# GroupNorm on one core: VectorE's loop unrolled over six ring slots, and two programs aligned with `addr_align`

## The chip, the cores and the metric

One core of one Trainium2 chip. The metric is the device time of one execution in microseconds (us). Every kernel is quoted by the median of its runs, with their range. A ratio "after over before" is the mean time of one kernel's fast runs over the mean of the other's fast runs of the same rounds on the same chip, so it is not quite the ratio of the quoted medians; it comes with a 95% interval.

The span of a run is what the profile covers, from the first to the last work on the core.

## The reference

GroupNorm in bf16 over an input of 128 x 1024 x 32 x 16, 32 groups of 32 channels:

```python
xr  = x.reshape(B, G, C // G, H, W)              # B=128, G=32, C=1024, H=32, W=16
mu  = xr.mean(axis=(2, 3, 4), keepdims=True)
var = ((xr - mu) ** 2).mean(axis=(2, 3, 4), keepdims=True)
xn  = (xr - mu) / jnp.sqrt(var + 1e-5)
return xn.reshape(B, C, H, W) * g[None, :, None, None] + b[None, :, None, None]
```

A row of one sample and one group has 32 x 512 = 16384 elements. 128 such rows make a tile of 4 MB, and there are 32 tiles. Every tile is read once and written once.

## The kernel before

Six ring slots of 4 MB hold the tiles. SyncE issues every large load and store into one DMA queue, in runs: some stores in a row, then as many loads in a row. The order is fixed by `RUNS`.

```python
SLOTS = 6
RUNS = (3, 4, 4, 4, 4, 4, 3, 6)
# ... cut ...
        for j in range(1, SLOTS):
            load(j)
        i = 0
        for run in RUNS:
            for n in range(run):
                store(i + n)
            i += run
            for j in range(i + SLOTS - run, min(i + SLOTS, NT)):
                load(j)
```

So the queue carries six loads, then tiles 0 to 2 out (tile 2 in two halves), tiles 6 to 8 in, tiles 3 to 6 out, tiles 9 to 12 in, and so on. A store is issued when VectorE has normalised its tile; a load when the store that last used its slot has landed.

Of a tile, PE sums one half (16 matmuls with an identity matrix), VectorE sums the other half by pairs, ScalarE forms the mean, two passes of squares and the root, and VectorE normalises in place with 32 instructions. ScalarE's program starts with two small loads of 2 KB, the gain and the bias:

```python
    def on_scalar(e):
        e.dma_start(out=gb_b[:, 0:KC], in_=g_v).then_inc(s_gb, 16)
        e.dma_start(out=gb_b[:, KC : 2 * KC], in_=b_v).then_inc(s_gb, 16)
        e.wait_ge(s_ones, 1)
        e.activation(out=warm[:], in_=eps_t[:], func=ACT.Sqrt)
    # ... cut: mean, squares, variance, root of each tile ...
    def on_tensor(e):
        e.wait_ge(s_eye, 2)
        e.wait_ge(s_gb, 32)
        e.matmul(out=gb_p[:], lhsT=rep[:], rhs=gb_b[:], start=True, stop=True).then_inc(s_gbp, 1)
        # ... cut ...
    def on_vector(e):
        # part(i, lo, n): a piece of slot i % SLOTS, at an address computed at run time
        e.wait_ge(s_gbp, 1)
        e.tensor_copy(out=gb[:], in_=gb_p[:])
        pair(0)
        with nc.Fori(0, NT, 1, engines=[e.engine]) as i:
            with e.If(i < NT - 1):
                e.drain()
                pair(i + 1)
            parts = [part(i, k * HW, HW) for k in range(KC)]
            e.keepalive_nop([e.lower_ap(a) for a in parts])
            e.wait_ge(stded, i + 1)
            # ... cut: 1/std, scale, shift, each with its semaphore ...
            for k, a in enumerate(parts):
                ts = e.tensor_scalar(
                    out=a, in0=a, scalar1=scl[:, k : k + 1], scalar2=bia[:, k : k + 1],
                    op0=ALU.mult, op1=ALU.add,
                )
                if (k + 1) % KQ == 0:
                    ts.then_inc(done, 1)
```

Of the kernel before, what the change touches and what calls it, by code (L numbers as in the profile page):

```python
# [8 lines left out]
ALU = mybir.AluOpType  # L9
F32 = mybir.dt.float32  # L10
BF16 = mybir.dt.bfloat16
# [5 lines left out]
SLOTS = 6  # L17
RUNS = (3, 4, 4, 4, 4, 4, 3, 6)
NQ = 4
PS_BUFS = 3  # L20
PE_CHUNKS = 16
MM_FREE = 512


# [33 lines left out]
def kernel(  # L58
# [13 lines left out]
    nc = tc.nc  # L72
# [3 lines left out]
    HW = H * W  # L76
# [3 lines left out]
    NT = B0 // NS  # L80
    KC = C // G
    F = KC * HW
    inv_n = 1.0 / float(F)
    NMM = F // MM_FREE
    ROUNDS = -(-NT // SLOTS)
    REST = NT - (ROUNDS - 1) * SLOTS
    KQ = KC // NQ
    PAIRED = F - PE_CHUNKS * MM_FREE
    ITEM = 2
    assert NT > SLOTS and 0 < REST < SLOTS and sum(RUNS) == NT and RUNS[-1] == SLOTS  # L90
    assert F % MM_FREE == 0 and PAIRED % 2 == 0 and SLOTS % PS_BUFS == 0

# [5 lines left out]
    def sbuf(name, shape, dtype):  # L98
        return nc.alloc_sbuf_tensor(name, shape, dtype)


    ring = sbuf("ring", [P, SLOTS * F], BF16)
    ja = sbuf("ja", [P, F // 2], FP8)
    jm = sbuf("jm", [P, MM_FREE + 1], FP8)
    jp = sbuf("jp", [P, PAIRED // 2], FP8)
# [4 lines left out]
    gb = sbuf("gb", [P, 2 * KC], F32)  # L110
    eps_t = sbuf("eps_t", [P, 1], F32)
    warm = sbuf("warm", [P, 1], F32)
    nm = sbuf("nm", [P, SLOTS], F32)
    sq = sbuf("sq", [P, 2], F32)
    var = sbuf("var", [P, 1], F32)
    std = sbuf("std", [P, SLOTS], F32)
    rstd = sbuf("rstd", [P, 1], F32)
    scl = sbuf("scl", [P, KC], F32)
    bia = sbuf("bia", [P, KC], F32)

    ps = nc.alloc_psum_tensor("ps", [P, PS_BUFS * 2 * MM_FREE], F32)
    gb_p = nc.alloc_psum_tensor("gb_p", [P, 2 * KC], F32)

    def sem(name):
        return nc.alloc_semaphore(name)

    def sems(name):
        return [sem(f"{name}{c}") for c in range(SLOTS)]

    ld, st, summed, meaned = (sems(n) for n in ("ld", "st", "sum", "mean"))  # L130

    half, both, varred = (sems(n) for n in ("half", "both", "var"))
    inverted, scaled, shifted = (sem(n) for n in ("inv", "scl", "bia"))
    first_in, paired, stded, done = (sem(n) for n in ("first", "pair", "std", "done"))
    s_gb, s_ones, s_eye, s_gbp, s_fin = (sem(n) for n in ("gbl", "ones", "eye", "gbp", "fin"))

    def store_parts(i):
# [2 lines left out]
    def slot(i):  # L140
        return ring[:, (i % SLOTS) * F : (i % SLOTS + 1) * F]
# [55 lines left out]
    def in_rounds(e, one):  # L197
        with nc.Fori(0, ROUNDS, 1, engines=[e.engine]) as t:
            for c in range(REST):
                one(c, t)  # L200
            with e.If(t < ROUNDS - 1):
                for c in range(REST, SLOTS):
                    one(c, t)
# [6 lines that stand above are left out]
        e.ldweights(eye[:])  # L210

        def add_up(to, chunk, k):
            return e.add_instruction(  # L213
                mybir.InstMatmult(
                    name=nc.get_next_instruction_name(),
                    engine=e.engine,
                    start_tensor_calc=(k == 0),
                    stop_tensor_calc=(k == PE_CHUNKS - 1),
                    ins=[e.lower_ap(chunk), e.lower_ap(eye[:])],
                    outs=[e.lower_ap(to)],  # L220
                    tile_size=(P, P),
                    tile_position=(0, 0),
                    ldweights=False,
                )
            )

        def one(c, t):
            for k in range(PE_CHUNKS):
                if k == 0:
                    e.wait_ge(ld[c], (t + 1) * 16)  # L230
                elif k == PE_CHUNKS - 2:

                    e.wait_ge(meaned[(c - 2) % SLOTS], t + 1)
                elif k == PE_CHUNKS - 1:
                    e.wait_ge(paired, t * SLOTS + (c + 1))
                mm = add_up(sums(c), slot(c)[:, k * MM_FREE : (k + 1) * MM_FREE], k)
                if k == 0:
                    mm.then_inc(first_in, 1)
            mm.then_inc(summed[c], 1)

        in_rounds(e, one)

    def on_scalar(e):
        e.dma_start(out=gb_b[:, 0:KC], in_=g_v).then_inc(s_gb, 16)
        e.dma_start(out=gb_b[:, KC : 2 * KC], in_=b_v).then_inc(s_gb, 16)
        e.wait_ge(s_ones, 1)
        e.activation(out=warm[:], in_=eps_t[:], func=ACT.Sqrt)  # L247

        def one(c, t):
            e.wait_ge(summed[c], t + 1)  # L250
            e.activation(  # L251
                out=jm[:], in_=sums_and_pairs(c), func=ACT.Identity, scale=-inv_n,
                accum_out=nm[:, c : c + 1], saturate=False,
            ).then_inc(meaned[c], 1)
            for h, (ready, at) in enumerate(
                ((meaned[c], t + (2 if c >= SLOTS - 2 else 1)), (half[c], t + 1))
            ):
                e.wait_ge(ready, at)
                e.activation(  # L259
                    out=ja[:],  # L260
                    in_=slot(c)[:, h * (F // 2) : (h + 1) * (F // 2)],
                    func=ACT.Square,
                    bias=nm[:, c : c + 1],
                    scale=1.0,
                    accum_out=sq[:, h : h + 1],
                    saturate=False,
                ).then_inc((half, both)[h][c], 1)
            e.wait_ge(both[c], t + 1)
            e.activation(  # L269
                out=var[:], in_=sq[:, 0:1], func=ACT.Identity, bias=eps_t[:], scale=inv_n  # L270
            ).then_inc(varred[c], 1)
            e.wait_ge(varred[c], t + 1)
            e.activation(  # L273
                out=std[:, c : c + 1], in_=sq[:, 1:2], func=ACT.Sqrt, bias=var[:], scale=inv_n
            ).then_inc(stded, 1)

        in_rounds(e, one)

    def on_vector(e):
        bytes_of_ring = ring[:].bitcast(mybir.dt.uint8)  # L280

        def part(i, lo, n):
            at = (i % SLOTS) * (F * ITEM) + lo * ITEM
            return bytes_of_ring[:, bass.ds(at, n * ITEM)].bitcast(BF16)

        def pair(i):
            lo, n = PE_CHUNKS * MM_FREE, PAIRED // 2
            e.wait_ge(first_in, i + 1)
            e.scalar_tensor_tensor(  # L289
                out=jp[:],  # L290
                in0=part(i, lo, n),
                scalar=1.0,
                in1=part(i, lo + n, n),
                op0=ALU.mult,
                op1=ALU.add,
                accum_out=ps[:, bass.ds((i % PS_BUFS) * (2 * MM_FREE) + MM_FREE, 1)],
                saturate=False,
            ).then_inc(paired, 1)

        e.wait_ge(s_gbp, 1)  # L300
        e.tensor_copy(out=gb[:], in_=gb_p[:])  # L301
        pair(0)
        with nc.Fori(0, NT, 1, engines=[e.engine]) as i:
            with e.If(i < NT - 1):
                e.drain()  # L305
                pair(i + 1)
            parts = [part(i, k * HW, HW) for k in range(KC)]
            e.keepalive_nop([e.lower_ap(a) for a in parts])  # L308
            e.wait_ge(stded, i + 1)
            e.reciprocal(out=rstd[:], in_=std[:, bass.ds(i % SLOTS, 1)]).then_inc(inverted, 1)  # L310
            e.wait_ge(inverted, i + 1)
            e.tensor_scalar(  # L312
                out=scl[:], in0=gb[:, 0:KC], scalar1=rstd[:], scalar2=None, op0=ALU.mult
            ).then_inc(scaled, 1)
            e.wait_ge(scaled, i + 1)
            e.scalar_tensor_tensor(  # L316
                out=bia[:], in0=scl[:], scalar=nm[:, bass.ds(i % SLOTS, 1)],
                in1=gb[:, KC : 2 * KC], op0=ALU.mult, op1=ALU.add,
            ).then_inc(shifted, 1)
            e.wait_ge(shifted, i + 1)  # L320
            for k, a in enumerate(parts):
                ts = e.tensor_scalar(  # L322
                    out=a, in0=a, scalar1=scl[:, k : k + 1], scalar2=bia[:, k : k + 1],
                    op0=ALU.mult, op1=ALU.add,
                )
                if (k + 1) % KQ == 0:
                    ts.then_inc(done, 1)

    with entry_block(tc) as entry:
        first_load(nc.sync)  # L330
# [3 lines left out]
        at = next(k for k, i in enumerate(rest) if is_drain(i) and i.engine == load_0.engine)  # L334
# [36 lines left out]
```

## Time and profile before

| | before |
|---|---|
| device time, first three runs | 630.39 us (630.19 to 630.68) |
| profiled span | 629.1 us |
| DMA share of the main queue | 99.3% |
| first tile store issued | 45.9 us |

The prediction below shows the lines from which the DMA bound is read (columns of a timeline: start and duration in us, engine, line, instruction; of the waits: who waits for whom, then total us, count, longest; of windows: window and length, busy us and count of PE, its weight loads, VectorE, ScalarE, GpSimd, then granted clock, DMA share, GB/s).

```profile
0.80 0.40 ACTq L244 DMA_DIRECT2D gb_b<-in_g_dram  x1
1.23 0.50 ACTq L245 DMA_DIRECT2D gb_b<-in_b_dram  x1
```

```profile
144.37 0.33 SPq L164 DMA_DIRECT2D out_dram<-ring  x1
144.74 14.54 SPq L158 DMA_DIRECT2D ring<-in_x_dram  x4
```

### The profile page before, as it was taken

Reading aid. Unit: us, or ns where it says so; the run is one execution under the profiler, and the core shown is the slowest. Engines: PE = TensorE matmul, PEld = TensorE weight load, DVE = VectorE, ACT = ScalarE, POOL = GpSimd, SP = SyncE. Lnnn points to the kernel's source line nnn. Section 1 sums busy time; section 2 is a strip of 40 time slices with the busy share of each in tenths; the row PEclk is TensorE's granted clock in tenths of the full one; section 3 lists DMA queues with packets and bytes.
Section 4 is the critical chain, followed back from the end, with each engine's and each line's share of the span. In section 5 each row is a group of like instructions: output and inputs, shape, how many; then the busy total and the mean of one; then the engine's idle time right before and its main releaser. Section 6 shows DMA issues by size and latency. Waiting matters only on the chain.

```text
span 629.1 us, 2702 instructions
## 1 busy us (share of the span) xinstructions
PE 187.5 (30%) x508; PEld 0.2 (0%) x2; DVE 497.2 (79%) x1185; ACT 504.0 (80%) x258; POOL 1.0 (0%) x8
## 2 busy tenths in 40 slices
PE   2533333430243303433024330343303333063000
PEld 0000000000000000000000000000000000000000
DVE  1479999999499982999829998299983999899962
ACT  0899999999589992999929999299991999979940
POOL 0000000000000000000000000000000000000000
PEclk9867766665577755777557775577755866577555
DMA  9999999999999999999999999999999999999996
GB/s 400 433 433 400 433 433 433 433 433 433 431 433 433 433 433 433 433 425 433 433 433 433 433 431 433 433 433 433 433 433 433 433 431 431 433 427 433 433 419 270
DMA packets 9888, 268.44 MB, mean 427 GB/s; under 512 B 1184, under 2 KB 1184, under 8 KB 1184
## 3 DMA queue, kind: packets, MB, share of 16 engines
q1 hardware_dynamic: 9792, 268.44, 99.3%
q10 hardware_dynamic: 96, 0.00, 0.0%
HBM read 134.22 MB, written 134.22 MB: 427 GB/s over the span
## 4 chain that ended last, share of the span: by engine, by line
ACT 32%; DVE 25%; DMA 24%; issue 9%; PE 4%; DVEq 3%; SPq 0%; ACTq 0%
ACT ja L259 30%; DVE ring L322 23%; DMA ring<-in_x_dram 22%; PE ps L213 4%; DMA gb_b<-in_b_dram 2%; ACT jm L251 1%; DVEq L305 1%; DVEq L308 1%; DVE jp L289 1%; ACT var L269 1%; ACT std L273 1%; DVE bia L316 1%; DVE scl L312 1%; DVEq L289 0%; DVE rstd L310 0%
## 5 line engine op out<-in xcount | busy, mean ns | idle before, releaser
L259 ACT ACTIVATE ja<-ring,nm 128x8192 fp8e5<-128x8192 bf16 x64 | 455.8, 7122 | 2.1
L322 DVE TENSOR_SCALAR ring<-ring,scl,bia x1024 | 333.7, 409 | 1.2
L213 PE MATMUL ps<-ring,eye 128*128 128x512 bf16 x507 | 187.3, 543 | 389.3 <-DVE jp L289 235.1
L289 DVE SCALAR_TENSOR_TENSOR jp<-ring 128x4096 fp8e5 (+1 forms) x32 | 141.6, 4425 | 80.9 <-PE ps L213 68.9
L251 ACT ACTIVATE jm<-ps 128x513 fp8e5<-128x513 f32 x32 | 19.2, 601 | 95.3 <-PE ps L213 95.3
L310 DVE RECIPROCAL rstd<-std 128x1 f32 x32 | 5.7, 177 | 19.3 <-ACT std L273 19.2
L259 ACT ACTIVATION_READ_ACCUMULATOR ja<-ring,nm 128x1 f32 x64 | 11.9, 186 | 0.0
L316 DVE SCALAR_TENSOR_TENSOR bia<-scl,nm,gb 128x32 f32<-128x32 f32 x32 | 8.0, 251 | 4.2
L301 DVE COPY gb<-gb_p 128x64 f32<-128x64 f32 x1 | 0.2, 225 | 12.8 <-PE gb_p L208 12.8
L273 ACT ACTIVATE std<-sq,var 128x1 f32<-128x1 f32 x32 | 9.4, 294 | 1.0
L269 ACT ACTIVATE var<-sq,eps_t 128x1 f32<-128x1 f32 x32 | 9.4, 295 | 1.0
L312 DVE TENSOR_SCALAR scl<-gb,rstd 128x32 f32<-128x32 f32 x32 | 7.7, 242 | 1.1
L251 ACT ACTIVATION_READ_ACCUMULATOR jm<-ps 128x1 f32 x32 | 6.2, 194 | 0.0
L289 DVE DVE_READ_ACCUMULATOR jp<-ring (+1 forms) x32 | 4.5, 142 | 0.0
L208 PE MATMUL gb_p<-gb_b,rep 32*128 32x64 bf16 x1 | 0.2, 208 | 12.5 <-DMA gb_b<-in_b_dram 12.5
L247 ACT ACT_TABLE_LOAD x1 | 1.3, 1283 | 1.8 <-PEq L355 1.8
L190 POOL TENSOR_SCALAR_AFFINE_SELECT rep<-ones_b 32x128 bf16<-32x128 bf16 x1 | 0.3, 303 | 0.0
L186 POOL TENSOR_SCALAR_AFFINE_SELECT eye<-ones_b 128x128 bf16<-128x128 bf16 x1 | 0.3, 293 | 0.4 <-issue 0.4
L247 ACT ACTIVATE warm<-eps_t 128x1 f32<-128x1 f32 x1 | 0.2, 203 | 0.0
L180 POOL MEMSET ones_b<- 128x128 bf16 x1 | 0.2, 204 | 0.3 <-POOLq L355 0.3
L210 PEld LDWEIGHTS <-eye 128*128 128x128 bf16 x1 | 0.1, 105 | 0.1
L208 PEld LDWEIGHTS gb_p<-gb_b,rep 32*128 32x128 bf16 x1 | 0.1, 100 | 12.5 <-issue 12.5
(5 smaller groups left out, 0.5 us busy)
## 6 DMA issues: line engine op xcount, KB each, us to landing
ring<-in_x_dram SPq DMA_DIRECT2D x32, 4096.0 KB, 36.8
out_dram<-ring SPq DMA_DIRECT2D x30, 4096.0 KB, 26.9
out_dram<-ring SPq DMA_DIRECT2D x2, 2048.0 KB, 12.5
out_dram<-ring SPq DMA_DIRECT2D x4, 1024.0 KB, 9.2
gb_b<-in_g_dram ACTq DMA_DIRECT2D x1, 2.0 KB, 7.8
gb_b<-in_b_dram ACTq DMA_DIRECT2D x1, 2.0 KB, 11.1
```

The lines of the kernel that those rows point to most:

```text
L213: return e.add_instruction(mybir.InstMatmult(name=nc.get_next_instruction_name(), engine=e.engine, start_tensor_calc=(k == 0), stop_tensor ...
L251: e.activation(out=jm[:], in_=sums_and_pairs(c), func=ACT.Identity, scale=-inv_n, accum_out=nm[:, c : c + 1], saturate=False,).then_inc(me ...
L259: e.activation(out=ja[:], in_=slot(c)[:, h * (F // 2) : (h + 1) * (F // 2)], func=ACT.Square, bias=nm[:, c : c + 1], scale=1.0, accum_out= ...
L269: e.activation(out=var[:], in_=sq[:, 0:1], func=ACT.Identity, bias=eps_t[:], scale=inv_n).then_inc(varred[c], 1)
L273: e.activation(out=std[:, c : c + 1], in_=sq[:, 1:2], func=ACT.Sqrt, bias=var[:], scale=inv_n).then_inc(stded, 1)
L289: e.scalar_tensor_tensor(out=jp[:], in0=part(i, lo, n), scalar=1.0, in1=part(i, lo + n, n), op0=ALU.mult, op1=ALU.add, accum_out=ps[:, bas ...
L305: e.drain()
L308: e.keepalive_nop([e.lower_ap(a) for a in parts])
L310: e.reciprocal(out=rstd[:], in_=std[:, bass.ds(i % SLOTS, 1)]).then_inc(inverted, 1)
L312: e.tensor_scalar(out=scl[:], in0=gb[:, 0:KC], scalar1=rstd[:], scalar2=None, op0=ALU.mult).then_inc(scaled, 1)
L316: e.scalar_tensor_tensor(out=bia[:], in0=scl[:], scalar=nm[:, bass.ds(i % SLOTS, 1)], in1=gb[:, KC : 2 * KC], op0=ALU.mult, op1=ALU.add,). ...
L322: ts = e.tensor_scalar(out=a, in0=a, scalar1=scl[:, k : k + 1], scalar2=bia[:, k : k + 1], op0=ALU.mult, op1=ALU.add,)
```

## The change

The intent is to take the loop turn, the run-time addresses and the drain off VectorE: the loop body handles the six slots with addresses fixed at build time, so it grows from 54 to 224 instructions (my count of the built program). The loop is aligned with `addr_align(FETCH)`, where `FETCH` is 128, and the code that runs once is put behind it and entered first. ScalarE's 49 instructions are aligned in the same way. That this alignment suits the fetching of instructions was my assumption; what the trace of before shows of fetches is nine packets of 8192 bytes, all outside the span. The counter semaphores become one per slot (54 semaphores become 78), and the pair sum waits for the load itself instead of PE's first matmul.

```diff
+FETCH = 128
-    inverted, scaled, shifted = (sem(n) for n in ("inv", "scl", "bia"))
-    first_in, paired, stded, done = (sem(n) for n in ("first", "pair", "std", "done"))
+    half, both, varred, inverted, scaled, shifted = (
+        sems(n) for n in ("half", "both", "var", "inv", "scl", "bia")
+    )
+    done = sem("done")
 ... cut: paired and stded become one per slot, PE's increment of first_in goes ...
     def on_scalar(e):
+        e.addr_align(FETCH, max_nops=0)
         e.dma_start(out=gb_b[:, 0:KC], in_=g_v).then_inc(s_gb, 16)
         e.dma_start(out=gb_b[:, KC : 2 * KC], in_=b_v).then_inc(s_gb, 16)
 ... cut ...
     def on_vector(e):
+        e.addr_align(FETCH, max_nops=0)
+        ahead = nc.cur_bb
+        nc.br("vector_fetch", engines=[e.engine])
+        nc.switch_bb("vector_start", parent=ahead)
+        def pair(c, turn):
+            e.wait_ge(ld[c], turn * 16)
 ... cut: the same pair sum, with static addresses ...
-        with nc.Fori(0, NT, 1, engines=[e.engine]) as i:
-            with e.If(i < NT - 1):
-                e.drain()
-                pair(i + 1)
-            parts = [part(i, k * HW, HW) for k in range(KC)]
-            e.keepalive_nop([e.lower_ap(a) for a in parts])
+        def one(c, t):
+            then = (c + 1) % SLOTS, t + (1 + (c + 1) // SLOTS)
+            if c == REST - 1:
+                with e.If(t < ROUNDS - 1):
+                    pair(*then)
+            else:
+                pair(*then)
 ... cut: 1/std, scale, shift, 32 normalising instructions on slot(c) ...
+        e.wait_ge(paired[0], 1)
+        in_rounds(e, one)
+        nc.br("vector_end", engines=[e.engine])
+        with nc.body("vector_fetch", parent=ahead, valid_engines=[e.engine]):
+            e.wait_ge(s_gbp, 1)
+            e.tensor_copy(out=gb[:], in_=gb_p[:])
+            pair(0, 1)
+            nc.br("vector_start", engines=[e.engine])
+        nc.switch_bb("vector_end")
```

## The prediction

What no trace of this case showed is cut from the text below and from two expectations (e8, e10), and each cut is marked. Among it is what the first rival was said to cost (a number of fetches in each round, and a time with them). The sum itself is 630.4 - 0 (VectorE) + 0 to 0.3 us (fetches), taken as 630.2 us. Of the fetch term, the 8 KiB and the 0.31 us are read from before's trace (packets of 8192 bytes, the undisturbed ones 307 to 324 ns); their number, one or two, was my estimate and does not follow from a trace.

> **What bounds the kernel now.** I read the page first: engine shares, then the slices, then the DMA queue. No compute engine is near full, but the DMA queue is.
>
> ```profile
> PE 187.5 (30%) x508; PEld 0.2 (0%) x2; DVE 497.2 (79%) x1185; ACT 504.0 (80%) x258; POOL 1.0 (0%) x8
> ...
> DMA  9999999999999999999999999999999999999996
> GB/s 400 433 433 400 433 433 433 433 433 433 431 433 433 433 433 433 433 425 433 433 433 433 433 431 433 433 433 433 433 433 433 433 431 431 433 427 433 433 419 270
> ...
> q1 hardware_dynamic: 9792, 268.44, 99.3%
> ```
>
> The reader is to see a flat 433 GB/s from the first slice to the one before the last. One tile is 4.194 MB in and 4.194 MB out, so at 433 GB/s a tile costs 8.389/433 = 19.37 us of DMA, and 32 tiles cost 619.9 us of the 629.1 us span. Only 9.2 us are left that any change of instructions could touch without moving fewer bytes.
>
> Next I read the waits, of the DMA queue's own engine and of all engines, because the chain of waits is mostly ACT (32%) and DVE (25%) and would mislead here: it follows what released each store, not whether the queue was ever empty.
>
> ```profile
> SPq L164 <- DVE ring L322: 472.9, 31, 42.4
> SPq L158 <- DMA out_dram<-ring: 112.0, 15, 9.6
> SPq L177 <- DMA out_dram<-ring: 11.1, 1, 11.1
> ...
> DVE jp L289 <- PE ps L213: 68.9, 8, 13.5
> DVE rstd L310 <- ACT std L273: 19.2, 16, 6.9
> ...
> DVE jp L289 <- issue: 12.0, 24, 0.5
> ```
>
> SyncE waits 472.9 us for VectorE before it issues stores. That looks like a VectorE bound, but in the table of DMA issues a 4 MB store lands 26.9 us (median) after its issue while it takes 9.7 us to move: about 17 us of earlier transfers stand ahead of it. A store issued some microseconds sooner only waits longer in the queue.
>
> Last, the timeline of VectorE and the end of the run in windows (columns: window and length, then busy us and count of each engine, granted clock, DMA share, GB/s).
>
> ```profile
> 555.29 0.20 DVE L310 RECIPROCAL rstd<-std 128x1 f32 x1
> ...
> 556.19 10.43 DVE L322 TENSOR_SCALAR ring<-ring,scl,bia  x32
> 567.12 4.43 DVE L289 SCALAR_TENSOR_TENSOR jp<-ring 128x4096 fp8e5 x1 [0.50 <-issue]
> ```
>
> ```profile
> 616.00:618.00 2.00, 0.00 (x0) 0.00 (x0) 0.64 (x2) 0.00 (x0) 0.00 (x0) 0.50 0.98 414
> ...
> 622.00:623.00 1.00, 0.00 (x0) 0.00 (x0) 0.00 (x0) 0.00 (x0) 0.00 (x0) 0.50 0.91 385
> 623.00:624.00 1.00, 0.00 (x0) 0.00 (x0) 0.00 (x0) 0.00 (x0) 0.00 (x0) 0.50 0.22 90
> ...
> 626.00:627.00 1.00, 0.00 (x0) 0.00 (x0) 0.00 (x0) 0.00 (x0) 0.00 (x0) 0.50 0.06 25
> 627.00:628.00 1.00, 0.00 (x0) 0.00 (x0) 0.00 (x0) 0.00 (x0) 0.00 (x0) 0.50 0.04 16
> ```
>
> The VectorE lines show a tile's cycle: from one pair-sum start at 550.94 to the next at 567.12 it is 16.18 us, 3.2 us less than the DMA needs. The window lines show two things. VectorE is done at 616.65, yet the DMA stays full for another 6 us: the last stores wait for the queue, not for VectorE. And from 624 us the share is 0.12, then 0.06, which is one engine of sixteen. So the span ends with one slow DMA engine that works alone from about 625 to 628.
>
> From the 16 semaphore increments of each transfer in the trace I followed that engine's distance behind the median of the sixteen: 0.37 us at 129 us, 1.39 at 245, 2.6 at 333, 3.7 at 478, 4.63 at the last store. It grows by about 0.1 us with every store, and by nothing with a load (1.39, 1.39, 1.40 over three loads from 245 to 265 us), apart from one jump of 0.7 us near 273.
>
> [...]the median increment of the last store is at 623.46 us and the last at 628.09.
>
> [...]The trace agrees with fetching by DMA[...]: its DMA records hold nine 8192-byte packets of the instruction kind[...], six before the first instruction, three after the last, and none in the 629 us between. Undisturbed ones took 307 to 324 ns. So the kernel before fetches nothing while it runs.
>
> [...]The trace has 0.50 us of issue time at the loop's turn, for a drain, two branches and register work together.
>
> **The change part by part.**
> Removed: per tile on VectorE, the drain, the loop turn, the dynamic addresses and the keepalive. The row of issue waits has 12.0 us in 24 turns, 0.5 us each; I expect 0.1 to 0.2 left, so 0.3 to 0.4 us of 32 tiles, 10 to 13 us of VectorE time in all. It takes the cycle from 16.2 to about 15.8 us. All of it lies beside a 19.37 us DMA tile: on the path, 0.
>
> Not changed: the 32 normalising instructions of a tile (10.43 us, 326 ns apart), the pair sum (4.43 us) and the three small ones. If static addresses also made issue faster, the 326 ns could shrink; no row of before tells, and it would be hidden too.
>
> Moved: the pair sum waits for the load itself and not for PE's first matmul. PE spent 235.1 us waiting for that sum, so PE and ACT may run some tenths of a microsecond earlier. Hidden, as ACT's cycle is about 16 us (2 squares of 7.25 us, 0.8 for the mean, 0.6 for the rest).
>
> Added: program. The loop grows from 54 instructions to 224 on VectorE (my count of the built program). [...]ScalarE's 49 instructions are only shifted. At the least one or two more 8 KiB fetches on some DMA engine, 0.31 us each; the start of VectorE's real work is at 12.75 us, so a fetch in the first microseconds is hidden.
>
> Sum: 630.4 - 0 (VectorE) + 0 to 0.3 (fetches, if they meet the slow engine). I take 630.2: the median, with a tenth or two off for a little less disturbance where loads turn to stores.
>
> **The rivals.**
> First, the loop is fetched anew in every round. [...]Against: the stall has 3.2 us per tile and a queue of 17 us to hide in, and an engine that is not the slow one stands more than 4 us ahead of it (two stand about 3). So 0 to 1 us[...].
>
> Second, the slow engine is slow because of something that the change removes, so that the tail of 4.6 us shrinks: 626 to 628. For it: the tail is the largest thing in the 9.2 us. Against: its delay comes in steps of 0.1 us with stores only, not in steps of 0.31 us once a round, and no fetch is recorded in the run.[...]
>
> Third, VectorE is on the path at the end: the last tile's work (605.35 to 616.65) delays the last store. Then 0.3 us could be gained, and a fetch stall would cost in full. Against: the queue is full to 622 us, so more than 4 us are spare.
>
> Fourth, the bubbles at load-to-store turns (the slice at 47 to 63 us with 400 GB/s lost about 1 us) change, since stores are issued at other moments: 1 us either way.
>
> **Range and chances.** The three times of before span 0.5 us. The bubbles give about 1 us either way, the second rival stretches downwards, the first a little upwards: 628.2 to 631.8. For 2% (12.6 us) down, more than the whole 9.2 us beside the transfers would have to go, which can't be; for 2% up, VectorE would have to fall behind the DMA by over 3 us in most tiles. Chances: 0.01 faster, 0.975 within 2%, 0.015 slower.
>
> **What would show it.** VectorE's issue wait before the pair sum falls from 12.0 us to under 5; its busy time stays near 497. The slices stay at 433 GB/s and the store's time to landing stays near 27 us or grows. The shares after 623 us keep their 0.06: if they are gone, my second rival is right. If instruction packets of 8192 bytes appear inside the run, the first rival's mechanism exists, and the slow engine's distance tells whether it counts. I'd be wrong altogether if slices in the middle fell under 420, which would mean that VectorE's stalls had emptied the queue.

## More of the kernel before

Where an experiment gives one span, it is that of its profiled run.

I number the large transfers from 0: loads 0 to 5, stores 6 to 9, loads 10 to 12, stores 13 to 16, loads 17 to 20. Transfer 16 is the store of tile 6.

```profile
PE gb_p L208 <- DMA gb_b<-in_b_dram: 12.5, 1, 12.5
```

ScalarE issues the two small loads in half a microsecond each, and the second lands late enough that PE starts only at 12.5 us. With it the work on the tiles begins.

```profile
117.00:119.00 2.00, 2.00 (x7) 0.00 (x0) 1.96 (x7) 1.90 (x3) 0.00 (x0) 0.50 0.84 360
...
148.00:150.00 2.00, 0.59 (x1) 0.00 (x0) 1.83 (x5) 1.01 (x4) 0.00 (x0) 0.50 1.07 459
...
158.00:160.00 2.00, 0.00 (x0) 0.00 (x0) 2.00 (x7) 2.00 (x1) 0.00 (x0) 0.50 0.87 377
...
197.00:199.00 2.00, 0.00 (x0) 0.00 (x0) 2.00 (x8) 1.97 (x3) 0.00 (x0) 1.00 0.91 393
```

In the timeline of SyncE's sequencer, the first line is the store of tile 6 alone, the second the four loads behind it. The store is issued by 144.70 us (144.37 + 0.33). By the semaphore increments in the trace, the store ahead of it lands at 148.56 us (median of its sixteen increments). So transfer 16 stands in the queue only 3.86 us before the queue would have nothing left. I call this distance the margin of a store. Of the stores before those of the last six tiles it is the smallest. The last store of each later run of four has 5.0 to 7.5 us, and the second half of tile 2 (transfer 9) has 6.73. Windows of 2 us swing by a packet or two, since the tool books a packet's bytes at its start; the four windows, at the store of tile 6 and at the turns from loads to stores before and after it, show a queue that does not stop.

```profile
144.84 4.42 DVE L289 SCALAR_TENSOR_TENSOR jp<-ring 128x4096 fp8e5 x1 [0.50 <-issue]
169.64 4.42 DVE L289 SCALAR_TENSOR_TENSOR jp<-ring 128x4096 fp8e5 x1 [9.13 <-PE ps L213]
```

The pair sums from 46 to 145 us wait only for issue: seven tiles in a row (2 to 8) are bound by compute, and what is late at their start is late at their end. The one at 169.64 us waits 9.13 us, for PE's first matmul on a tile whose load has just landed. From there on the queue sets VectorE's clock, and a late start is forgotten.

## The result, and the profile after

| | before | after |
|---|---|---|
| device time, six runs each, same chip | 630.29 us (630.10 to 630.72) | 631.73 us (631.09 to 632.80) |
| ratio after over before | | 1.0025 [1.0012, 1.0038] |
| time outside the span, mean | 1.52, 1.58 and 1.60 us (nine runs on each of three later chips) | 1.90 us (six runs) |

The changed kernel is 0.25% slower: within 2%, but clearly apart, and above what I had allowed. The means of the runs are 631.93 and 630.36 us (the latter from the before runs of the same chip), 1.57 us apart. About 0.3 to 0.4 of it lies outside the span, which leaves about 1.2 us in the span. The profiled run of after was its slowest (632.80 us, span 630.9; the other five spans are 629.2 to 630.8), and the profiled span of before is 629.1, so what is read from these two traces, 1.8 us in the span, is larger than what a typical run lost.

The page of after, in the lines that answer to those of before (the rows with a q are a queue and its kind: packets, MB, share of the 16 engines' time):

```profile
PE 183.8 (29%) x508; PEld 0.2 (0%) x2; DVE 495.7 (79%) x1185; ACT 503.2 (80%) x258; POOL 1.0 (0%) x8
...
GB/s 397 432 432 403 432 426 432 422 434 432 407 432 428 432 432 432 432 432 432 432 432 432 432 432 430 432 432 430 434 432 436 432 428 432 432 436 432 436 423 279
...
q1 hardware_dynamic: 9792, 268.44, 99.3%
...
q14 instruction: 3, 0.02, 0.0%
```

The queue is as full as before, with slices of 426, 422, 407 and 428 where before had 431 to 433. Each slice is 15.8 us long, so these lie at about 79 to 95, 110 to 126, 158 to 174 and 189 to 205 us. A new row counts three instruction packets inside the span; before had none.

VectorE did gain what the change is for. The timeline of one tile's cycle, and the waits of SyncE, follow:

```profile
516.30 4.45 DVE L294 SCALAR_TENSOR_TENSOR jp<-ring 128x4096 fp8e5<-128x4096 bf16 x1
...
521.72 10.43 DVE L327 TENSOR_SCALAR ring<-ring,scl,bia 128x512 bf16<-128x512 bf16 x32
532.03 4.45 DVE L294 SCALAR_TENSOR_TENSOR jp<-ring 128x4096 fp8e5<-128x4096 bf16 x1
```

```profile
SPq L170 <- DVE ring L327: 472.5, 31, 48.0
SPq L164 <- DMA out_dram<-ring: 113.1, 14, 9.4
```

From pair sum to pair sum it is 15.73 us instead of 16.18, and the issue wait of 12.0 us before the pair sum has no row any more. Yet SyncE's waits for VectorE are the same to half a microsecond in total (472.5 for 472.9), and its longest wait, the one for the first store (the last number of the line), grew from 42.4 to 48.0 us. That points to the start of the run:

```profile
1.24 6.12 ACTq L249 DMA_DIRECT2D gb_b<-in_g_dram  x1
7.38 0.44 ACTq L250 DMA_DIRECT2D gb_b<-in_b_dram  x1
```

```profile
PE gb_p L214 <- DMA gb_b<-in_b_dram: 17.5, 1, 17.5
```

The issue of the first small load takes 6.12 us instead of 0.40. The second goes out at 7.38 us instead of 1.23, its data land about 5 us later, PE starts at 17.5 us instead of 12.5, and the first tile store is issued at 51.5 us instead of 45.9. Inside the 6.12 us lie two of the three instruction packets (at 5.29 and 5.62 us; 309 ns each; 8192 bytes). They went to the DMA while the first tile loads were under way: six had been issued by 3.17 us, and the first of them landed at 12.13 us (median of its sixteen increments). One of the two belongs to VectorE's alignment, as e1 and e2 below tell (packets at 5.68 and 11.40 us without ScalarE's alignment, a single one at 5.41 with it alone).

What a late start does to a queue that is "full" is seen at the store of tile 6 (the columns are those of before):

```profile
147.62 0.33 SPq L170 DMA_DIRECT2D out_dram<-ring  x1
147.99 14.49 SPq L164 DMA_DIRECT2D ring<-in_x_dram  x4
```

```profile
117.00:119.00 2.00, 0.00 (x0) 0.00 (x0) 2.00 (x1) 2.00 (x1) 0.00 (x0) 0.50 0.95 262
...
148.00:150.00 2.00, 0.00 (x0) 0.00 (x0) 2.00 (x1) 2.00 (x1) 0.00 (x0) 0.50 0.80 344
...
158.00:160.00 2.00, 0.00 (x0) 0.00 (x0) 2.00 (x8) 2.00 (x1) 0.00 (x0) 0.50 0.69 295
...
197.00:199.00 2.00, 1.19 (x5) 0.00 (x0) 2.00 (x7) 2.00 (x1) 0.00 (x0) 0.90 0.53 229
```

The store is issued 3.25 us later than in before. Of the 5.6 us that the first store was late, the shorter cycle has made good 2.3 by then. The margin of tile 6's store is 1.52 us instead of 3.86; that of transfer 9 is 1.72 us instead of 6.73. And the window at 117 us moved 262 GB/s for 360 in before, those at 158 and 197 us 295 and 229 for 377 and 393.

The margin of tile 6 is 1.52 us, that of transfer 9 is 1.72. The landings tell what this costs. I took the median of the sixteen increments of every large transfer from the two traces:

| transfer | what | lands, before, us | after minus before, us |
|---|---|---|---|
| 11 | load of tile 7 | 109.82 | -0.04 |
| 12 | load of tile 8 | 119.54 | +0.81 |
| 15 | store of tile 5 | 148.56 | +0.91 |
| 16 | store of tile 6 | 158.62 | +1.16 |
| 17 | load of tile 9 | 167.91 | +1.27 |
| 19 | load of tile 11 | 187.33 | +1.27 |
| 20 | load of tile 12 | 197.03 | +1.94 |
| 28 | load of tile 16 | 274.69 | +1.87 |
| 36 | load of tile 20 | 352.26 | +1.80 |
| last | last store | 623.46 | +1.87 |

The loss comes in three pieces: 0.85 us between transfers 11 and 12, where loads give way to stores; 0.36 us from transfer 15 to 17, at tile 6's store; 0.67 us between 19 and 20, the next turn from loads to stores. At the first and the last of these the trace shows 32 KiB packets of up to 2.8 and 3.0 us where one takes 1.21 otherwise; the packets of before take no more than 1.41 us at those turns. By the packets no DMA engine of after stands idle around these places: summed over the sixteen engines, there is no gap from 76 to 122 us or from 140 to 204 us. So the queue of after never ran dry; what it lost, it lost in packets that took longer.

So all that after lost at the median engine it lost before 200 us, and it stayed lost. The distance of the slowest engine behind the median at the last store is 4.83 us, for 4.63 in before. The tail is as long, but not of one engine alone:

```profile
625.00:626.00 1.00, 0.00 (x0) 0.00 (x0) 0.00 (x0) 0.00 (x0) 0.00 (x0) 0.50 0.19 82
...
628.00:629.00 1.00, 0.00 (x0) 0.00 (x0) 0.00 (x0) 0.00 (x0) 0.00 (x0) 0.50 0.12 49
```

Shares of 0.19 and 0.12 are three engines and two, where before had one at 0.06. At the store of tile 29 the three slowest stand 4.91, 4.09 and 3.06 us behind the median, for 4.54, 1.71 and 1.31 in before.

### The profile page after: what moved, and what is told of

The parts are those of the page before. It is cut to its first block, busy times and chain, and to the rows that moved or that the text cites. A ratio compares the mean times of both kernels' runs of the same rounds, so it can differ in the third digit from the quotient of the medians.

```text
span 630.9 us, 2170 instructions
## 1 busy us (share of the span) xinstructions
PE 183.8 (29%) x508; PEld 0.2 (0%) x2; DVE 495.7 (79%) x1185; ACT 503.2 (80%) x258; POOL 1.0 (0%) x8
## 3 DMA queue, kind: packets, MB, share of 16 engines
q1 hardware_dynamic: 9792, 268.44, 99.3%
## 4 chain that ended last, share of the span: by engine, by line
ACT 35%; DMA 34%; DVE 20%; PE 6%; issue 1%; ACTq 1%; SPq 0%; DVEq 0%
ACT ja L264 32%; DMA ring<-in_x_dram 22%; DVE ring L327 16%; DMA out_dram<-ring 11%; PE ps L219 6%; DVE jp L294 3%; DMA gb_b<-in_b_dram 2%; ACT jm L256 1%; ACTq L249 1%; ACT var L274 1%; ACT std L278 1%; DVE bia L320 0%; DVE scl L316 0%; DVE rstd L314 0%; SPq L170 0%
## 5 line engine op out<-in xcount | busy, mean ns | idle before, releaser
L327 DVE TENSOR_SCALAR ring<-ring,scl,bia 128x512 bf16<-128x512 bf16 x1024 | 333.7, 420 | 1.2
L219 PE MATMUL ps<-ring,eye 128*128 128x512 bf16 x507 | 183.6, 535 | 388.4 <-DVE jp L294 227.7
L294 DVE SCALAR_TENSOR_TENSOR jp<-ring 128x4096 fp8e5<-128x4096 bf16 x32 | 142.1, 4440 | 64.5 <-DMA ring<-in_x_dram 64.5
L314 DVE RECIPROCAL rstd<-std 128x1 f32<-128x1 f32 x32 | 5.5, 170 | 35.4 <-ACT std L278 34.3
L339 DVE COPY gb<-gb_p 128x64 f32<-128x64 f32 x1 | 0.2, 225 | 17.7 <-PE gb_p L214 17.7
L214 PE MATMUL gb_p<-gb_b,rep 32*128 32x64 bf16 x1 | 0.2, 207 | 17.5 <-DMA gb_b<-in_b_dram 17.5
L294 DVE DVE_READ_ACCUMULATOR jp<-ring 128x1 f32 x32 | 5.2, 162 | 0.0
L214 PEld LDWEIGHTS gb_p<-gb_b,rep 32*128 32x128 bf16 x1 | 0.1, 100 | 17.5 <-issue 17.5
```

The lines of the kernel that those rows point to most:

```text
L219: return e.add_instruction(mybir.InstMatmult(name=nc.get_next_instruction_name(), engine=e.engine, start_tensor_calc=(k == 0), stop_tensor ...
L294: e.scalar_tensor_tensor(out=jp[:], in0=slot(c)[:, first : first + w], scalar=1.0, in1=slot(c)[:, first + w : first + 2 * w], op0=ALU.mult ...
L314: e.reciprocal(out=rstd[:], in_=std[:, c : c + 1]).then_inc(inverted[c], 1)
L327: ts = e.tensor_scalar(out=a, in0=a, scalar1=scl[:, k : k + 1], scalar2=bia[:, k : k + 1], op0=ALU.mult, op1=ALU.add,)
```

## The experiments

The theory after reading the two traces: **the late start.** ScalarE's alignment makes it jump to instructions that, I supposed, are not yet loaded; the fetch of them, I supposed further, waits among the load packets (e4 below corrects this); the small loads go out 6 us late; all compute is 5 us late; the margins of the early stores are used up, and the queue loses time there and at the turns that follow. The rivals: **the fetches**, which cost the DMA engine that serves them, through VectorE's alignment as much as ScalarE's; and **the static loop**, which by itself issues stores at less favourable moments. In the expectations these stand under their own names: theory F is the alignment's fetch at ScalarE's start, with a late-start branch and an engine branch; rival S is the static loop; theory M says that late work uses up the margin of a store; rival T that a late start costs by itself at the turns. (They speak of a stall of the second small load; the traces show it in the issue of the first.)

Kernel before was run with each group on the same chip: 630.55 us (nine runs) with e1 to e4, 630.66 with e5 to e8, 630.49 with e9 to e11. All kernels gave correct results.

### e1: the change without ScalarE's alignment

```diff
     def on_scalar(e):
-        e.addr_align(FETCH, max_nops=0)
         e.dma_start(out=gb_b[:, 0:KC], in_=g_v).then_inc(s_gb, 16)
```

> The changed kernel without ScalarE's alignment; VectorE's static loop and its alignment stay. Theory F (the fetch at ScalarE's start: it stalls the second gain/bias load for 6 us and two 8 KiB instruction packets set DMA engines back): no 6 us issue on ScalarE, at most one instruction packet inside the span, the early distance of the slowest DMA engine back to about 0.3 us from 1.5, time 630.1 to 630.6. Rival S (the static VectorE loop itself, or its own fetches, cost the time): 631.3 to 632, as the changed kernel. Part of both: the time outside the span stays 0.3 us above before, if it comes from the added semaphores.

Measured: 631.28 us (630.93 to 631.49), ratio 1.0009 [0.9995, 1.0023], span 629.5. That lies above theory F's 630.6 and just under rival S's 631.3. The two issues are back at 0.40 and 0.53 us, PE starts at 14.2 us, and the margin of tile 6 is 3.70 us. The median landing of the last store is 0.40 us earlier than in before, so the loss in the queue is gone. But the time is 0.7 us above before's median, because the slowest engine ends 5.67 us behind the median, a microsecond more than in before. It is 2.04 us behind already early in the run (0.3 was expected), after the two remaining instruction packets (5.68 and 11.40 us; one at most was expected). An engine that far behind would also explain why PE does not start at 12.5 us: the last completion of the two small loads comes at 13.59 us, the one before it at 12.14, for 11.97 and 11.89 in before. So the late start explains the queue's loss; this kernel keeps something else, at its end, and its interval does not tell that from nothing.

### e2: before, with ScalarE's alignment alone

```diff
     def on_scalar(e):
+        e.addr_align(128, max_nops=0)
         e.dma_start(out=gb_b[:, 0:KC], in_=g_v).then_inc(s_gb, 16)
```

> The kernel before with ScalarE's alignment added, nothing else. Theory F: the 6 us stall at the second gain/bias load appears, one or two instruction packets in the first 12 us, time 631.0 to 632. Rival S: the stall may appear, but the time stays at 630.1 to 630.7.

Measured: 632.64 us (631.69 to 633.07), ratio 1.0029 [1.0015, 1.0042], span 631.2. One line, which changes no arithmetic and no order, costs 2.1 us, a little more than the 632 expected at most. The issue in the timeline, and the window at tile 6's store:

```profile
1.23 5.72 ACTq L245 DMA_DIRECT2D gb_b<-in_g_dram  x1
```

```profile
148.00:150.00 2.00, 0.00 (x0) 0.00 (x0) 1.50 (x5) 2.00 (x1) 0.00 (x0) 0.60 0.00 0
```

The stall is there with a single instruction packet (at 5.41 us); PE starts at 16.7 us. With the old loop the margin is -0.40 us: the store comes after the previous one has landed, and no packet starts in these 2 us. The median landing of the last store is 3.52 us later than in before, the slowest engine 3.25 us behind it. The loss therefore doesn't need the static loop, which if anything softens it (1.4 us in after).

### e3: before, with the second small load late and no fetch

```diff
         e.dma_start(out=gb_b[:, 0:KC], in_=g_v).then_inc(s_gb, 16)
+        e.wait_ge(s_gb, 16)
         e.dma_start(out=gb_b[:, KC : 2 * KC], in_=b_v).then_inc(s_gb, 16)
```

> The kernel before, in which ScalarE waits for its first small load to land before it issues the second: the first tile's work starts at about 17.5 us and not 12.7, as in the changed kernel, but nothing is fetched. If the late start is what costs (theory F, late-start branch): 631 to 632, with bubbles where loads turn to stores. If the fetch packets' delay of single DMA engines is what costs (theory F, engine branch): 630.1 to 630.7 and no early distance of 1.5 us.

Measured: 631.89 us (631.25 to 632.39), ratio 1.0017 [1.0003, 1.0031], span 630.7. PE starts at 16.3 us. The margin of tile 6 is -0.43 us and the queue runs dry without a single fetch (by the packets, the engines stand idle for 1.3 us on average):

```profile
148.00:150.00 2.00, 0.00 (x0) 0.00 (x0) 1.50 (x3) 2.00 (x1) 0.00 (x0) 0.50 0.62 262
...
158.00:160.00 2.00, 0.00 (x0) 0.00 (x0) 2.00 (x8) 2.00 (x1) 0.00 (x0) 0.50 0.46 180
```

The landings shift by +1.54 us at transfer 16, +1.99 at 17 and +2.96 at 20, and stay at +2.92 to the end. So being late is enough. Two further things are seen. The loss has another part at the next turn from loads to stores, near 196 us, 0.95 us by the excess of its packets, although the margins there are back above 20 us. And not all of it reaches the end: the slowest engine is only 3.39 us behind at the last store, 1.24 less than in before, so a dry queue also lets the slow engine catch up.

### e4: the change, with ScalarE's alignment behind the two small loads

```diff
     def on_scalar(e):
-        e.addr_align(FETCH, max_nops=0)
         e.dma_start(out=gb_b[:, 0:KC], in_=g_v).then_inc(s_gb, 16)
         e.dma_start(out=gb_b[:, KC : 2 * KC], in_=b_v).then_inc(s_gb, 16)
+        e.addr_align(FETCH, max_nops=0)
         e.wait_ge(s_ones, 1)
```

> The changed kernel with ScalarE's two small loads issued ahead of the alignment: the fetch stays, but the first tile no longer starts late (12.7 us). Late-start branch: back to 630.1 to 630.7. Engine branch: stays at 631.2 to 632, with the early distance of 1.5 us. Rival S: stays as well, even without that distance.

Measured: 630.68 us (630.43 to 631.22), ratio 1.0004 [0.9990, 1.0017], span 628.5: level with before.

```profile
0.80 0.40 ACTq L248 DMA_DIRECT2D gb_b<-in_g_dram  x1
```

```profile
q14 instruction: 3, 0.02, 0.0%
```

```profile
158.00:160.00 2.00, 0.00 (x0) 0.00 (x0) 1.13 (x4) 2.00 (x1) 0.00 (x0) 0.50 0.95 410
```

It makes the same number of fetches, at nearly the same moments (5.64, 5.81 and 11.36 us), and even keeps a slow engine 1.97 us behind early in the run. Only the small loads no longer stand behind the alignment: PE starts at 14.2 us (not at the expected 12.7, as in e1), and the margins of transfers 9 and 16 are 6.09 and 4.90 us. After is 1.44 us above its own before, this kernel 0.13 us above its own, so 1.3 of the 1.44 us come from the order of three lines (the interval of e4 is 0.8 us to each side). This is the clearest of the runs: it keeps the fetches and the static loop, and takes away most of the late start. It also corrects the theory in one place. After the alignment's branch, which the trace has at 1.76 us, ScalarE goes on at once:

```profile
2.20 1.28 ACT L252 ACT_TABLE_LOAD   x1 [2.20 <-issue]
```

That is 0.44 us after the branch and 3.4 us before the first instruction packet, so ScalarE did not stand waiting for the instructions to which it jumped. In e2 too the branch (0.79 us) is followed after 0.44 us by the issue of the small load; it is this issue that then takes 5.72 us.

### e5: the late start of e3, with the run of stores shortened

If the loss is the fourth store of the second run, an order that asks for three stores there should not lose it.

```diff
-RUNS = (3, 4, 4, 4, 4, 4, 3, 6)
+RUNS = (3, 3, 4, 4, 4, 4, 4, 6)
 ... and the wait of e3 ...
```

> The kernel with the late second load (which cost 1.3 us) with one more change: the second run of stores has three instead of four, so that the store of tile 6 no longer has to be issued before 149 us with an almost empty queue. Theory M (late work eats the queue's margin at that store, 3.9 us in the kernel before, none with the late start): the queue does not run dry near 149 to 160 us, slices there back at 433 GB/s, time 630.2 to 631.0. Rival T (a late start costs by itself, through the load-to-store turns near 117 and 197 us): time stays at 631.3 to 632.4.

Measured: 630.67 us (630.33 to 631.26), ratio 1.0001 [0.9987, 1.0014], span 629.3. The start is as late as in e3, and the loss is gone: at transfer 62 the landing is 0.05 us earlier than in before, where e3 is 2.91 us later. The new order changes the end as well (the queue empties among the last stores, and the engines end within 0.47 us of each other), so the last 10 us are not comparable, but in this kernel, whose margin at transfer 9 was still 3.00 us, the loss before 200 us is a matter of that one store. This rests on the landings: the intervals of e3's and e5's ratios overlap.

### e6: before, later still

```diff
         e.dma_start(out=gb_b[:, 0:KC], in_=g_v).then_inc(s_gb, 16)
+        e.wait_ge(ld[0], 16)
         e.dma_start(out=gb_b[:, KC : 2 * KC], in_=b_v).then_inc(s_gb, 16)
```

> Dose: the kernel before with the second small load held until the whole first tile has landed (12.2 us), so the first tile's work starts at about 20 us, 7 to 8 us late instead of 5. Theory M: each further microsecond beyond the margin costs one: the store of tile 6 is issued 2 to 3 us later than with the first dose, time 634 to 636. Rival T: the loss does not grow with the dose, 631.5 to 632.7.

Measured: 636.71 us (636.52 to 637.17, four fast runs), ratio 1.0098 [1.0082, 1.0113]; more than I expected, because I had counted on tile 6's store. The window shows a queue that is dry already at the halves of tile 2:

```profile
80.00:82.00 2.00, 0.57 (x3) 0.00 (x0) 2.00 (x7) 2.00 (x1) 0.00 (x0) 1.00 0.00 0
```

The margins of transfers 7 to 9 are 0.58, -0.90 and 0.68 us, and the landings shift by +2.25 us at transfer 8, +3.36 at 10, +5.74 at 16 and +7.03 at 20, then no more. Beyond the first margin, being late costs on more than one turn.

### e7: the change, with the run of stores shortened

```diff
-RUNS = (3, 4, 4, 4, 4, 4, 3, 6)
+RUNS = (3, 3, 4, 4, 4, 4, 4, 6)
```

> The changed kernel with the second run of stores cut to three as well. Theory M: the 0.4 us at 150 to 170 us are gone, time 630.6 to 631.3 with about 0.3 us of it outside the span. Rival T: 631.5 to 632.5, bubbles near 117 and 197 us remain.

Measured: 631.58 us (630.54 to 632.94), ratio 1.0011 [0.9997, 1.0024]. Inconclusive: by its time it falls to rival T (631.5 to 632.5), by its interval it may be level with before. The loss between 149 and 170 us is nearly gone and so is the one near 197, but the one near 117 us stays (1.0 us, after a margin of 1.51 us at transfer 9), and the slowest engine is 5.9 us behind at the store of tile 29. The runs spread over 2.4 us.

### e8: the static loop alone, with neither alignment

```diff
     def on_scalar(e):
-        e.addr_align(FETCH, max_nops=0)
 ...
     def on_vector(e):
-        e.addr_align(FETCH, max_nops=0)
-        ahead = nc.cur_bb
-        nc.br("vector_fetch", engines=[e.engine])
-        nc.switch_bb("vector_start", parent=ahead)
 ...
+        e.wait_ge(s_gbp, 1)
+        e.tensor_copy(out=gb[:], in_=gb_p[:])
+        pair(0, 1)
         e.wait_ge(paired[0], 1)
         in_rounds(e, one)
-        nc.br("vector_end", engines=[e.engine])
-        with nc.body("vector_fetch", parent=ahead, valid_engines=[e.engine]):
 ... the four lines of the entry block, now above, are cut ...
-        nc.switch_bb("vector_end")
```

> VectorE's static loop with neither alignment nor the entry from the last block. If the alignment is needed, instruction packets show up in every round of the loop[...], each setting one DMA engine back by about 0.9 us: slowest engine 8 us or more behind at the end, time 634 or more. If all of the loop stays loaded anyway: one or two packets at the start, time 630.5 to 631.3, as the version without ScalarE's alignment.

Measured: 630.69 us (630.34 to 631.21), ratio 1.0003 [0.9989, 1.0016], span 628.6: level with before. PE starts at 12.5 us as in before. The margin of tile 6 is 6.44 us, the best with this order, and buys nothing, since before's 3.86 were enough. The page has the row

```profile
q14 instruction: 3, 0.02, 0.0%
```

of which two are 8192-byte packets, at 46.64 and 103.33 us, both while the loop goes through its six slots for the first time, and the third is one of 40 bytes. It does not fetch in every round. So the alignment and the entry block of VectorE save nothing that these runs show.

### e9: before, made to run dry elsewhere

To see whether the second part of the loss follows a dry queue, whatever made it dry, this order asks for five stores in the second run, with nothing late.

```diff
-RUNS = (3, 4, 4, 4, 4, 4, 3, 6)
+RUNS = (3, 5, 3, 4, 4, 4, 3, 6)
```

> The kernel before with five stores in the second run instead of four (and three in the third), no late start: the store of tile 7 has to be issued near 161 us, when the transfer ahead of it lands at about 158.6. Theory M with its second half (a queue that has run dry once pays a further 0.5 to 1 us where loads next turn to stores): the queue is dry for 2 to 5 us near 160 us, and the next turn, near 210 us, has a bubble of 0.5 us or more that the kernel before doesn't have; part comes back in the tail, as the slow engine is caught up; time 632 to 635. Rival T (the bubbles belong to a late start): dry near 160, but no bubble at the next turn.

Measured: 635.23 us (634.64 to 635.91), ratio 1.0071 [1.0058, 1.0085], span 634.2. The fifth store has a margin of -3.55 us:

```profile
158.00:160.00 2.00, 0.00 (x0) 0.00 (x0) 2.00 (x8) 1.97 (x3) 0.00 (x0) 0.50 0.00 0
160.00:162.00 2.00, 0.00 (x0) 0.00 (x0) 1.30 (x5) 2.00 (x1) 0.00 (x0) 0.50 0.00 0
...
221.00:223.00 2.00, 0.96 (x3) 0.00 (x0) 1.80 (x6) 0.67 (x3) 0.00 (x0) 0.50 0.69 295
```

It is 5.24 us later than before at transfer 17, and loses another 0.65 us at the next turn from loads to stores, at 218.8 to 220.6 us. So the second loss follows the dry place; it is no property of a moment in the run.

### e10 and e11: an attempt at the tail

Of before's span the last 4.6 us belong to one slow DMA engine. I split the last two stores of 1 MB into partitions 0 to 119 and 120 to 127, in the hope that the slow engine would be spared, in before (e10) and on top of e8 (e11).

```diff
-                e.dma_start(
-                    out=o_v[i][:, p * w : (p + 1) * w], in_=slot(i)[:, p * w : (p + 1) * w]
-                ).then_inc(st[i % SLOTS] if i + SLOTS < NT else s_fin, 16)
+                for lo, hi in ((0, 120), (120, P)) if i == NT - 1 and p >= 2 else ((0, P),):
+                    e.dma_start(
+                        out=o_v[i][lo:hi, p * w : (p + 1) * w],
+                        in_=slot(i)[lo:hi, p * w : (p + 1) * w],
+                    ).then_inc(st[i % SLOTS] if i + SLOTS < NT else s_fin, 16)
```

> The kernel before with the last two megabytes of the last tile stored as 120 and 8 partitions[...]. If the slow engine of the tail is the sixteenth: its distance at the end falls from 4.6 us to under 2.5, time 628.0 to 629.0, faster than both kernels. If it is another: 630.4 to 631.2, tail unchanged or a little longer.

> VectorE's static loop without alignments, with the same split of the last two megabytes. If the slow engine is the sixteenth: 628.0 to 629.2, level with the split on the kernel before, which would show that the static loop is worth nothing either way; else 630.5 to 631.3.

Measured: e10 634.82 us (634.53 to 635.04), ratio 1.0068 [1.0054, 1.0081]; e11 635.93 us (634.76 to 636.11), ratio 1.0084 [1.0071, 1.0098]. Both failed by over 4 us: in e10 one engine works alone from 626 to 632 us (shares of 0.06 and 0.07), in e11 about two do (0.16 to 0.11). That the split spares one engine, "the sixteenth" of the expectations, was my assumption. What the trace shows is 14 packets more in the main queue (9806 for 9792): 23 completion packets in place of 16 for each of the two stores. By the chain of packets in the trace, the slow engine got eight packets of each large piece and one of each small piece besides. So the split did not spare it. Two more packets of 0.31 us do not make 4 us; where the rest comes from is open.

### The runs side by side

A margin is the median landing of the transfer ahead, less the end of the store's own issue. The loss near 117 us is the excess of the slow packets over 1.21 us, shared by 16 engines. The last column is the median landing of the last store against before's, each in its profiled run (e5 and e7 have another order, so none is given).

| kernel | time, us | ratio | PE starts, us | margin, transfer 9 | loss near 117 us | margin, tile 6 | last store |
|---|---|---|---|---|---|---|---|
| before | 630.29 | 1 | 12.5 | 6.73 | none | 3.86 | 0 |
| e8 static loop alone | 630.69 | 1.0003 | 12.5 | 7.71 | 0.08 | 6.44 | -0.21 |
| e4 alignment behind the loads | 630.68 | 1.0004 | 14.2 | 6.09 | 0.01 | 4.90 | -0.11 |
| e1 no ScalarE alignment | 631.28 | 1.0009 | 14.2 | 5.00 | 0.01 | 3.70 | -0.40 |
| e5 late, shorter run | 630.67 | 1.0001 | 16.1 | 3.00 | 0.01 | moved | |
| e3 late, no fetch | 631.89 | 1.0017 | 16.3 | 2.36 | 0.08 | -0.43 | +2.92 |
| e2 alignment alone | 632.64 | 1.0029 | 16.7 | 1.93 | 0.47 | -0.40 | +3.52 |
| after | 631.73 | 1.0025 | 17.5 | 1.72 | 1.00 | 1.52 | +1.87 |
| e7 after, shorter run | 631.58 | 1.0011 | 17.7 | 1.51 | 1.00 | moved | |
| e6 later still, no fetch | 636.71 | 1.0098 | 20.8 | 0.68 | 0.95 | -0.01 | +7.15 |

The column of losses near 117 us follows the margin of transfer 9: at most 0.08 us at 2.36 us and above, half a microsecond at 1.93, a whole one at 1.72 and below. e6 has it without any fetch. Only part of this is a dry queue. In e2 and e3 the landing of a store comes about 0.3 us after the median engine's last packet, and the next store's first packet about 0.5 us after the end of its issue. So by my estimate from these two figures a gap opens only under a margin of about 0.8 us. At 1.5 to 1.9 us the queue is close to empty but no engine idles; why the packets of the next turn then take longer is not shown.

No version here beats both kernels. The versions that keep the order and have margins of 3.7 us and more lose nothing in the queue; all with a margin under 2 us do.

## Why the prediction was wrong

**What held.** The DMA queue bounds both kernels (its packets fill 99.3% of the span in each). VectorE's gain came about in its size (the cycle from 16.18 to 15.73 us; the issue wait from 12.0 us to no row), and it is hidden: e8, the static loop alone, is level with before. The busy times are as foretold, and the tail neither shrank nor vanished, though more engines share it. The first rival (a fetch in every round), the second (a shorter tail) and the third (VectorE on the path at the end) did not happen: the last store of after is issued 5.75 us before the transfer ahead of it lands. One sign of being wrong altogether did come true, a slice in the middle under 420 (407 at 158 to 174 us), but not through stalls of VectorE.

**The step that failed** is the one on the added program: "ScalarE's 49 instructions are only shifted", and "a fetch in the first microseconds is hidden". ScalarE was not only shifted: the alignment put a branch ahead of its first useful instruction, with a fetch of instructions soon after, and the issue of its first small load then took 6.12 us instead of 0.40. I had looked for the cost at VectorE's start, which waits until 12.75 us anyway. But VectorE waits there for PE, and PE for the small loads of ScalarE. The start time that I used as a shelter was itself at the end of the chain that the alignment lengthened, from 12.5 to 17.5 us at PE. e2 (the alignment alone, +2.1 us) and e4 (as many fetches, the alignment behind the small loads, level) show this from both sides. What holds the issue for 6 us is not shown. That it waits for a fetch which itself waits among the load packets is inferred from the moment of the packet (5.41 us in e2, while the issue lasts from 1.23 to 6.95); e4 speaks against a wait for the branch's target.

**A second step hid its consequence.** I took "about 17 us of earlier transfers" ahead of a store as slack for any delay. That is a median over 30 stores. The margin that counts is the smallest, and it was to be read in the kernel before: 3.86 us at the store of tile 6, and 6.73 at transfer 9. Both belong to the stretch in which VectorE waits for no load, so that a late start reaches them almost in full; the later stores start from a load and do not feel it. e3 (late without a fetch, dry) and e5 (as late, but without that store in its run, no loss) show it for the kernel before. In after the larger part, 0.85 and 0.67 us, lies at the turns; that it comes of the late start is shown by e4, the way from a small margin to slow packets is not.

**A term was mis-sized.** I put a fetch at 0.31 us of one DMA engine, the packet itself. The trace of after shows the 32 KiB packets that start as its three fetches end taking 1.63 to 1.88 us instead of 1.21, so by my estimate from these a fetch costs its engine about 0.7 to 1.0 us (0.31 plus the 0.42 to 0.66 added). An engine is 1.6 to 2.0 us late early in after, e1 and e4, after two to three fetches. It did not decide the time: e4 has it and is level.

**The fourth rival was real, but with the wrong size and cause.** I allowed 1 us either way for turns, as chance. In the profiled run two turns cost 0.85 and 0.67 us and tile 6's store 0.36, all in one direction and all after stores with small margins; the kernels with larger margins (e1, e4, e8) have none of the three to speak of (0.08 us at most). The typical run of after lost less (mean span 630.0 us), so the sizes vary from run to run. Together with the 0.3 to 0.4 us outside the span, which I had not foreseen at all, they take the time to the upper end of the range, 631.8: the median of 631.73 us lies just inside, the mean of 631.93 just outside, and so is before's 630.39 times the ratio (631.97).

**What stays open.** Why a turn costs 0.6 to 1 us after the queue has been dry or nearly so is not settled; e9 shows only that it follows. Why e1's slowest engine ends 5.67 us behind, when e4's, as far behind early, ends at 4.48, is not known; it grows in steps of up to 1 us at turns from loads to stores in both. The static kernels spend more time outside their span: 1.72 us in e1 and e8, 1.85 to 1.90 in after, e4 and e7, for 1.52 to 1.60 in before. That may come from the longer program or from the 24 more semaphores; no run separates them. In the span e4 and e8 are level with before or a shade shorter (means of 628.94 for 629.11, and 628.98 for 629.11 us).

## What to carry to other kernels

A full queue is not slack: before you call a delay hidden, find the store with the smallest time between its issue and the landing of the transfer ahead of it, and compare the delay with that one (3.86 us here) and not with the median (about 17 us). Put alignment and code placement behind the first small loads that other engines wait for, and look at the start in the trace: in e4 this took away 3.3 of the 5.0 us of late start. And ask of a start time that seems to give shelter which chain sets it, and whether the change lengthens that chain.
